# Slot 1 of the routed feed-forward filled from the first three pairs of batches

## The chip, the core and the metric

The kernel runs on one core of a Trainium2 chip. Five engines work on it at once, each through its own list of instructions in order: PE (TensorE, matrix products; its weight loads are shown apart as PEld), DVE (VectorE), ACT (ScalarE), POOL (GpSimd) and SP (SyncE, which issues most of the DMAs). An instruction starts when the one before it on its engine allows it and when the semaphores that it waits for have come. The metric is the device time of one execution in microseconds (us); lower is better. PE's clock has two levels, 2.4 and 1.2 GHz; the profile writes the granted one as a share of the full clock, 1.00 or 0.50, and a mean over a stretch in between.

## What is computed

Attention with two softmaxes, a routed feed-forward with one of 8 experts for each token, and a gated feed-forward over all tokens:

```python
q_s = softmax(q, axis=-1)                    # q, k, v: 8 batches x 8 heads x 576 x 64
k_s = softmax(k, axis=2)                     # over the sequence
kv  = einsum('bhsd,bhse->bhde', k_s, v)
x   = einsum('bhsd,bhde->bhse', q_s, kv)     # -> 4608 tokens x 512
logits = x @ w_gate + modality_bias[modality_id]
e_idx, gate_w = argmax(logits), softmax(logits)[e_idx]
for e in range(8):                           # w1: 8 x 512 x 1024, w2: 8 x 1024 x 512
    out[e_idx == e] = gate_w * (relu(x[e_idx == e] @ w1[e]) @ w2[e])
y = ((out @ w_a) * (out @ w_b)) @ w_out      # w_a, w_b: 512 x 1536, w_out: 1536 x 512
```

## The kernel before

**Stages.** First the attention, in 16 units (`u`: a batch and one half of its heads), software-pipelined by the list `STEP`: in each turn every step runs for another unit. After every second batch (a *pair*: 1152 tokens, 9 columns of 128) the pair is routed. The routing is a generator that `more` advances a few operations at a time among the attention's steps: logits, the one-hot choice `oh`, the rank of each token within its expert (running counts are in `carry`), and for each column two matrices `la` and `lb` that carry the token numbers. When a pair is done, `("route", n)` is set and a hook `then[n]` is called, if there is one.

**Slots.** The routed feed-forward runs in slots of 256 tokens, all of one expert. Each slot gathers its tokens (two indirect DMAs on POOL's queue, `gather`, 128 rows each, from `xd`, the attention's output in DRAM), scales them by row (`xscale` on DVE, four small operations for each half: `xm`, `xp`, `xr`, `fc`; `xmul` on ACT), transposes them on PE (`xtrans`), splits them into a high and a low part of 16 bits (`xsplit`: high on ACT, low on DVE, into `xhl`), multiplies by w1 (`ph`, 96 products; in slot 0 `pt`), makes `hh` (ACT) and `hl` (DVE) of that for each of 8 blocks, multiplies by w2 (`py`; in slot 0 `po`), and scales the sum on ACT (`ysb`) for the store to `yd`. 19 slots run. The *leader* is the expert that has most tokens after the first pair (`plan_first`, `c.first`). Slot 0 takes the first 256 of the leader's tokens and is worked beside the attention's last units, slot 1 the next 256.

**Which tokens are slot 0's and slot 1's.** `Plan.first` decides that. `rank`, called after the second pair, lifts the leader's running count to at least 256 (`max(256, carry)`), so that no later token gets a rank that slot 0 has; how far it was lifted is `phi`. `mark(n, s)` makes a one-hot table `eq` (in the tile `tables`) over the first `n` columns: which leader's tokens have the ranks of slot `s`. `products(n)` multiplies it by `la` and `lb` of each column, 2 `n` small products on PE into `pid`, and `index(s)` turns that into the row numbers `gidx` that the gather reads. For slot 0 `n` is 18 (two pairs); for slot 1 it is 36, all columns, so the chain waits for the last pair's routing. `Plan.tokens` does the same for all other slots, as four times 18 products (`pid<-eqs`).

**What sets the order.** The slot-0 and slot-1 work is cut into chains of small steps; a step is put into the program at a `tick` of the attention once its conditions are in `gone` and the count of ticks has reached its number in the table `AT` (third row: slot 1's chain, whose 15 steps are `mark`, products, `index`, the gather, scaling, transposes and splits). From slot 2 on the class `Work` puts the conversions of weights and the steps of `Plan.tables` (it writes the table of slots, with each slot's base from `phi` and the counts) one by one into the engines' lists, by their costs and due times; another step in its list moves what is behind it.

**After the slots** comes the gated feed-forward (`Gated`), 9 blocks of 512 tokens, which is over half of the time and keeps PE busy.

Some names: `kvb` is the small matrix of a unit that its output products (`po<-kvb,qt`) use, `psg` the sum it comes from; `w_91` and `w_92` are the expert's w1 and w2 in 16 bits, of which DVE makes the low part and POOL, ACT and DVE the high one; `hot` is the one-hot table from which ACT makes `la` and `lb`; `x` and `xs` are the attention's output tiles.

Of the kernel before, what the change touches and what calls it, by code (L numbers as in the profile page):

```python
# [13 lines left out]
ALU = mybir.AluOpType  # L14
AX = mybir.AxisListType
# [4 lines left out]
B, H, S, D = 8, 8, 576, 64  # L20
NTOK = B * S
# [15 lines left out]
class Attention:  # L37
# [368 lines left out]
    def more(self, n):  # L406

        while n > 0 and self.todo is not None:
# [16 lines left out]


# [162 lines left out]
class Plan:  # L589
# [18 lines left out]
    def first(self, at):  # L608

        nc, c, v = self.nc, self.c, self.nc.vector  # L610
        t8, self.phi = self.tile(2, NE), self.tile(1)
        hs, hi = self.tile(NT, NE), self.tile(NT)
        self.hs = hs.rearrange("p n e -> p (n e)")
        eq = self.tile(NT).bitcast(F16).rearrange("p (n two) -> p n two", two=2)

        def rank():
            v.scalar_tensor_tensor(t8[:, 0], c.first, float(SLOT), c.carry, ALU.mult, ALU.max)
            v.tensor_tensor(t8[:, 1], t8[:, 0], c.carry, ALU.subtract)
            v.tensor_copy(c.carry, t8[:, 0])
            v.tensor_reduce(self.phi, t8[:, 1], AX.X, ALU.add)  # L620
            mark(18, 0)

        def mark(n, s):
            v.tensor_tensor(hs[:, 0:n], c.oh[:, 0:n], c.first[:, None, :].to_broadcast([P, n, NE]), ALU.mult)
            v.tensor_reduce(hi[:, 0:n], hs[:, 0:n], AX.X, ALU.add)
            v.scalar_tensor_tensor(hi[:, 0:n], hi[:, 0:n], -1000.0, c.hir[:, 0:n], ALU.mult, ALU.add)
            v.tensor_tensor(eq[:, 0:n], hi[:, 0:n, None].to_broadcast([P, n, 2]),
                            c.is1000[:, None, 2 * s:2 * s + 2].to_broadcast([P, n, 2]), ALU.is_equal)

        def products(n):  # L630
            self.ps = at.ps_t.tile([P, 2], F32, tag="pt", name="pid0")
            for j in range(n):
                nc.tensor.matmul(self.ps, c.la[:, j], eq[:, j], start=j == 0, stop=False)
                nc.tensor.matmul(self.ps, c.lb[:, j], eq[:, j], start=False, stop=j == n - 1)

        def index(s):
            v.tensor_scalar(c.gidx[:, 2 * s:2 * s + 2], self.ps, -65.0, 0.0, ALU.add, ALU.max)

        return (rank, [([("route", 1), ("kmax_t", 13)], lambda: products(18)), ((), lambda: index(0)), ((), lambda: at.gone.add("0"))],
                [([("route", NT // 9 - 1), "0"], lambda: mark(NT, 1)), ((), lambda: products(NT)), ((), lambda: index(1))])  # L640

    def tokens(self, at):

# [45 lines left out]
    def tables(self, done):  # L689
# [48 lines left out]
        v.tensor_reduce(bs, g, AX.X, ALU.add)  # L738
        yield one
        v.scalar_tensor_tensor(bs, c.iota50[:, 0:MAXSLOT], float(SLOT), bs, ALU.mult, ALU.add)  # L740
        yield one
        v.tensor_scalar(c.plan[:, BASE:BASE + MAXSLOT], bs, self.phi, float(NTOK), ALU.subtract, ALU.min)
        yield one
# [111 lines left out]
class Experts:  # L855
# [165 lines left out]
    def gather(self, s, j):  # L1021
        nc, c = self.nc, self.c
        nc.gpsimd.indirect_dma_start(  # L1023
            out=self.x[:, j], out_offset=None, in_=self.xd[0:4 * S if s == 0 else NTOK, :],
            in_offset=bass.IndirectOffsetOnAxis(ap=c.gidx[:, 2 * s + j:2 * s + j + 1], axis=0))

    def xscale(self, h):
# [926 lines left out]
def moe_kernel(ctx: ExitStack, tc: tile.TileContext, q, k, v, mid, wg, mb, w1, w2, wa, wb, wo, out, dbg=None):  # L1954
# [8 lines left out]
    with ExitStack() as ectx:  # L1963
        ex = Experts(tc, ectx, c, xd, yd, wd, w1, w2)
        plan = Plan(tc, ectx, c)
        with ExitStack() as rctx:
            load_modality, token_bias = setup_tokens(tc, rctx, c, mid, wg, mb)
            with ExitStack() as actx:
                at = Attention(tc, actx, c, q, k, v, xd, ex)
                rank, *tokens = plan.first(at)  # L1970
                early = [*ex.early(at, *tokens), plan.tokens(at)]
                at.run({0: [load_modality], 3: [token_bias]}, {0: lambda: plan_first(tc, c, at.one), 1: rank}, early)
        if dbg is not None and dbg.get("stop") == "T":
            return
        gctx = ectx.enter_context(ExitStack())
        with ExitStack() as sctx:
            gt = Gated(tc, gctx, sctx, c, dr, ex, plan, wa, wb, wo, out)
            ex.open(sctx)
            if dbg is not None and dbg.get("stop") == "L":
                return  # L1980

            def planned():
                ex.planned = True

            ex.work.add(plan.tables(planned))
            ex.run(gt)
        if dbg is not None:
            nc.sync.dma_start(out=dbg["x"], in_=xd)
            nc.sync.dma_start(out=dbg["plan"], in_=c.plan)
            nc.sync.dma_start(out=dbg["gidx"], in_=c.gidx)  # L1990
            nc.sync.dma_start(out=dbg["y"], in_=yd[0:NTOK, :])
            if dbg.get("stop") == "B":
                return
        gt.open(gctx)
        gt.run()
# [31 lines left out]
```

## Time and profile before

| | us |
|---|---|
| median of 3 runs | 1415.15 |
| lowest, highest | 1412.2, 1416.22 |
| the profiled execution | 1412.71 |
| its span in the trace | 1410.7 |
| PE busy in the span | 1343.4 (95%) |
| DVE busy | 1051.7 (75%) |
| ACT busy | 676.4 |
| POOL busy | 561.1 |

The span is the trace's own time; 2.0 us of the execution lie around it. A line of the timeline has the start, the duration, the engine, the line of the program, the operation, what it writes and reads, shapes and the count; in brackets the idle time of its engine just before it and what ended that. Products overlap in PE's pipeline, so that the next may start before the end shown.

### The profile page before, as it was taken

Reading aid. Unit: us, or ns where it says so; the run is one execution under the profiler, and the core shown is the slowest. Engines: PE = TensorE matmul, PEld = TensorE weight load, DVE = VectorE, ACT = ScalarE, POOL = GpSimd, SP = SyncE. Lnnn points to the kernel's source line nnn. Section 1 sums busy time; section 2 is a strip of 40 time slices with the busy share of each in tenths; the row PEclk is TensorE's granted clock in tenths of the full one; section 3 lists DMA queues with packets and bytes.
Section 4 is the critical chain, followed back from the end, with each engine's and each line's share of the span. In section 5 each row is a group of like instructions: output and inputs, shape, how many; then the busy total and the mean of one; then the engine's idle time right before and its main releaser. Section 6 shows DMA issues by size and latency. Waiting matters only on the chain.

```text
span 1410.7 us, 29129 instructions
## 1 busy us (share of the span) xinstructions
PE 1343.4 (95%) x11068; PEld 1106.5 (78%) x11068; DVE 1051.7 (75%) x2342; ACT 676.4 (48%) x1625; POOL 561.1 (40%) x696
## 2 busy tenths in 40 slices
PE   6887899999999999999999999999999999999996
PEld 4776776666676776768888888888888888888885
DVE  6889876776787777426777878788787877878755
ACT  4566563764455554323545354454443545454433
POOL 6655431524443354103334343433434334343433
PEclk9988799999999999999999999999999999999999
DMA  9987234789654345117001010100101001010000
GB/s 245 269 261 218 85 129 146 268 310 310 225 199 155 108 135 165 61 47 292 1 18 45 1 61 2 61 1 1 61 1 61 1 17 46 1 61 1 32 1 31
DMA packets 87911, 145.79 MB, mean 103 GB/s; under 512 B 19792, under 2 KB 60752, under 8 KB 85584
## 3 DMA queue, kind: packets, MB, share of 16 engines
q1 hardware_dynamic: 81136, 123.85, 27.2%
q0 software_dynamic: 6080, 19.95, 4.3%
q8 instruction: 90, 1.47, 0.4%
q14 instruction: 61, 0.50, 0.1%
q10 hardware_dynamic: 544, 0.02, 0.0%
HBM read 149.78 MB, written 46.44 MB: 139 GB/s over the span
## 4 chain that ended last, share of the span: by engine, by line
PE 52%; issue 1%; DVE 1%; POOL 1%; ACT 0%; POOLq 0%; DVEq 0%
PE ab L1654 34%; PE mp L1674 17%; PE ab L1338 1%; POOL out_dram L1748 0%; ACT y L1333 0%; POOLq L2022 0%; DVE g L1903 0%; DVE y L1348 0%; POOL raw L1693 0%; DVE w L1903 0%; DVE w L1358 0%; DVE g L1906 0%; DVE gr L1902 0%; POOL gs L1780 0%; POOL w L1693 0%
## 5 line engine op out<-in xcount | busy, mean ns | idle before, releaser
L1654 PEld LDWEIGHTS <-gw 128*128 128x128 f16 x3780 | 369.5, 98 | 53.2 <-issue 8.9
L1654 PE MATMUL ab<-raw,gw 128*128 128x256 f16 x2100 | 280.4, 272 | 3.7 <-DVE w L1906 1.1
L1654 PE MATMUL ab<-w,gw 128*128 128x256 f16 x1680 | 225.2, 273 | 0.2
L1674 PEld LDWEIGHTS <-gp 128*128 128x128 f16 x1944 | 190.0, 98 | 22.6 <-DVE gp L1701 0.8
L1061 PEld LDWEIGHTS <-w 128*128 128x128 f16 x1824 | 179.4, 99 | 31.6 <-issue 6.5
L1061 PE MATMUL ph<-xhl,w 128*128 128x256 f16 x1728 | 195.7, 274 | 4.7 <-DVE hl L1069 2.4
L1078 PE MATMUL py<-w,hh 128*128 128x512 f16 x576 | 171.3, 379 | 0.1
L1674 PE MATMUL mp<-wo,gp 128*128 128x256 f16 x756 | 141.8, 273 | 0.0
L1701 DVE SCALAR_TENSOR_TENSOR gp<-gp,gs 128x256 f16<-128x256 f16 x162 | 88.9, 553 | 36.8 <-ACT gp L1696 36.5
L1069 DVE SCALAR_TENSOR_TENSOR hl<-ph,hh 128x256 f16<-128x256 f32 x144 | 59.1, 420 | 72.7 <-ACT hh L1068 69.5
L1078 PE MATMUL py<-w,hl 128*128 128x512 f16 x288 | 109.1, 379 | 0.0
L1078 PEld LDWEIGHTS <-hh 128*128 128x128 f16 x608 | 59.5, 99 | 61.6 <-issue 0.3
L1470 POOL TENSOR_TENSOR gf<-gf 128x256 f32<-128x256 f32 x72 | 64.1, 910 | 94.7 <-ACT gf L1513 86.2
L1696 ACT ACTIVATE gp<-g 128x256 f16<-128x256 f32 x108 | 45.0, 418 | 98.8 <-DVE g L1906 97.9
L1732 POOL TENSOR_TENSOR gs<-w 128x256 f32<-128x256 f32 x54 | 39.6, 734 | 125.8 <-DVE w L1906 125.8
L1674 PE MATMUL mp<-w,gp 128*128 128x256 f16 x324 | 88.3, 273 | 0.0
L1674 PE MATMUL mp<-raw,gp 128*128 128x256 f16 x324 | 88.3, 273 | 0.0
L1068 ACT ACTIVATE hh<-ph 128x256 f16<-128x256 f32 x144 | 54.3, 379 | 68.3 <-PE ph L1061 67.8
L1701 DVE SCALAR_TENSOR_TENSOR gp<-gp,g 128x256 f16<-128x256 f16 x108 | 74.2, 688 | 15.8 <-ACT gp L1696 15.7
L1023 POOL DMA_INDIRECT xg<-xd,gidx x40 | 44.4, 1111 | 98.6 <-ACT xhl L1052 51.6
L1654 PEld LDWEIGHTS <-w 128*128 128x128 f16 x756 | 73.9, 98 | 10.1 <-issue 0.7
L1893 ACT COPY gr<-ab 128x256 f32<-128x256 f32 x108 | 40.3, 373 | 86.5 <-PE ab L1654 86.0
(358 smaller groups left out, 2740.0 us busy)
## 6 DMA issues: line engine op xcount, KB each, us to landing
w<-wd SPq DMA_DIRECT2D x58, 1024.0 KB
raw<-in_moe_w_dram SPq DMA_DIRECT2D x24, 512.0 KB
yd<-ysb SPq DMA_DIRECT2D x19, 513.0 KB
xd<-x SPq DMA_DIRECT2D x8, 1026.0 KB
y<-yd SPq DMA_DIRECT2D x8, 1026.0 KB
w<-in_k_dram SPq DMA_DIRECT2D x16, 512.0 KB
wd<-wst SPq DMA_DIRECT2D x16, 512.0 KB
g<-in_moe_w_a_dram SPq DMA_DIRECT2D x12, 512.0 KB
```

The lines of the kernel that those rows point to most:

```text
L1023: nc.gpsimd.indirect_dma_start(out=self.x[:, j], out_offset=None, in_=self.xd[0:4 * S if s == 0 else NTOK, :], in_offset=bass.IndirectOffs ...
L1061: nc.tensor.matmul(ph, self.w1[:, w, k, o], x[:, k], start=i == 0, stop=i == 11)
L1068: nc.scalar.activation(self.hh[:, f], ph, AF.Relu)
L1069: nc.vector.scalar_tensor_tensor(self.hl[:, f], ph, 0.0, self.hh[:, f], ALU.max, ALU.subtract)
L1078: nc.tensor.matmul(self.py[j], h[:, f, o], self.w2[:, w, f], start=f == 0 and i == 0, stop=f == 7 and i == 2)
L1470: self.nc.gpsimd.tensor_tensor(s[:, dst], s[:, x], s[:, y], ALU.subtract)
L1654: self.nc.tensor.matmul(ps, self.w[f][:, b, o:o + P], self.y[n].op[:, a, yl, 256 * k:256 * k + 256], start=i == 0 and fresh, stop=i == 5, ...
L1674: self.nc.tensor.matmul(onto[:, t], x, y, start=start and j == 0, stop=i == last and t == 1 and j == 2, skip_group_check=nm == "p3" and al ...
L1696: self.nc.scalar.activation(self.part(i, a)[:, 0], x, AF.Copy, scale=2.0 ** -11)
L1701: eng.scalar_tensor_tensor(p[:, 1], p[:, 0], -2048.0, x, ALU.mult, ALU.add)
L1732: pool.tensor_tensor(x, a11, a21, ALU.subtract)
L1893: nc.scalar.copy(r, x)
```

## The change

The running count of the leader is shifted a second time, after the third pair: `later` lifts it to at least 512, by the same four operations as `rank` (`shift(s)`), and adds the two lifts (`gap`) up to `phi`. With that, slot 1's ranks lie within the first three pairs. `mark` and `products` of slot 1 run over 27 columns, not 36, and wait for the third pair's routing, not the last one's; its gather reads rows of the first 6 batches only. The third row of `AT` has earlier numbers, and `Plan.tables` adds slot 1's own lift to its base, which is one more step in `Work`'s list.

With this input the leader has 595 tokens after the first pair and 1146 after the third: both lifts are zero, and slot 1 gets the same tokens as before.

```diff
--- before.py
+++ after.py
@@ -420,7 +420,7 @@
           (505, 509, 509, 509, 509, 552, 557, 565, 574, 574, 587, 596, 619, 623, 643, 648, 649, 650, 650, 653,
            654, 660, 667, 667, 668, 668, 668, 668, 670, 670, 670, 676, 676, 676, 679, 679, 679, 679,
            679, 696, 738, 765),
-          (643, 643, 648, 653, 691, 694, 696, 702, 702, 711, 711, 711, 715, 715, 740),
+          (618, 622, 628, 648, 650, 660, 665, 668, 671, 677, 677, 678, 680, 681, 683),
           (637, 659, 662, 704, 708, 714, 714, 714, 714, 718, 724))
 
 
@@ -608,17 +608,24 @@
     def first(self, at):
 
         nc, c, v = self.nc, self.c, self.nc.vector
-        t8, self.phi = self.tile(2, NE), self.tile(1)
+        t8, self.phi, self.gap = self.tile(2, NE), self.tile(1), self.tile(2)
         hs, hi = self.tile(NT, NE), self.tile(NT)
         self.hs = hs.rearrange("p n e -> p (n e)")
         eq = self.tile(NT).bitcast(F16).rearrange("p (n two) -> p n two", two=2)
 
-        def rank():
-            v.scalar_tensor_tensor(t8[:, 0], c.first, float(SLOT), c.carry, ALU.mult, ALU.max)
+        def shift(s):
+            v.scalar_tensor_tensor(t8[:, 0], c.first, float(SLOT * (s + 1)), c.carry, ALU.mult, ALU.max)
             v.tensor_tensor(t8[:, 1], t8[:, 0], c.carry, ALU.subtract)
             v.tensor_copy(c.carry, t8[:, 0])
-            v.tensor_reduce(self.phi, t8[:, 1], AX.X, ALU.add)
+            v.tensor_reduce(self.gap[:, s:s + 1], t8[:, 1], AX.X, ALU.add)
+
+        def rank():
+            shift(0)
             mark(18, 0)
+
+        def later():
+            shift(1)
+            v.tensor_reduce(self.phi, self.gap, AX.X, ALU.add)
 
         def mark(n, s):
             v.tensor_tensor(hs[:, 0:n], c.oh[:, 0:n], c.first[:, None, :].to_broadcast([P, n, NE]), ALU.mult)
@@ -636,8 +643,8 @@
         def index(s):
             v.tensor_scalar(c.gidx[:, 2 * s:2 * s + 2], self.ps, -65.0, 0.0, ALU.add, ALU.max)
 
-        return (rank, [([("route", 1), ("kmax_t", 13)], lambda: products(18)), ((), lambda: index(0)), ((), lambda: at.gone.add("0"))],
-                [([("route", NT // 9 - 1), "0"], lambda: mark(NT, 1)), ((), lambda: products(NT)), ((), lambda: index(1))])
+        return (rank, later, [([("route", 1), ("kmax_t", 13)], lambda: products(18)), ((), lambda: index(0)), ((), lambda: at.gone.add("0"))],
+                [([("route", 2), "0"], lambda: mark(27, 1)), ((), lambda: products(27)), ((), lambda: index(1))])
 
     def tokens(self, at):
 
@@ -738,6 +745,8 @@
         v.tensor_reduce(bs, g, AX.X, ALU.add)
         yield one
         v.scalar_tensor_tensor(bs, c.iota50[:, 0:MAXSLOT], float(SLOT), bs, ALU.mult, ALU.add)
+        yield one
+        v.tensor_tensor(bs[:, 1:2], bs[:, 1:2], self.gap[:, 1:2], ALU.add)
         yield one
         v.tensor_scalar(c.plan[:, BASE:BASE + MAXSLOT], bs, self.phi, float(NTOK), ALU.subtract, ALU.min)
         yield one
@@ -1021,7 +1030,7 @@
     def gather(self, s, j):
         nc, c = self.nc, self.c
         nc.gpsimd.indirect_dma_start(
-            out=self.x[:, j], out_offset=None, in_=self.xd[0:4 * S if s == 0 else NTOK, :],
+            out=self.x[:, j], out_offset=None, in_=self.xd[0:(4 + 2 * s) * S if s < 2 else NTOK, :],
             in_offset=bass.IndirectOffsetOnAxis(ap=c.gidx[:, 2 * s + j:2 * s + j + 1], axis=0))
 
     def xscale(self, h):
@@ -1967,9 +1976,9 @@
             load_modality, token_bias = setup_tokens(tc, rctx, c, mid, wg, mb)
             with ExitStack() as actx:
                 at = Attention(tc, actx, c, q, k, v, xd, ex)
-                rank, *tokens = plan.first(at)
+                rank, later, *tokens = plan.first(at)
                 early = [*ex.early(at, *tokens), plan.tokens(at)]
-                at.run({0: [load_modality], 3: [token_bias]}, {0: lambda: plan_first(tc, c, at.one), 1: rank}, early)
+                at.run({0: [load_modality], 3: [token_bias]}, {0: lambda: plan_first(tc, c, at.one), 1: rank, 2: later}, early)
         if dbg is not None and dbg.get("stop") == "T":
             return
         gctx = ectx.enter_context(ExitStack())
```

Where the instructions stand. PE at the attention's last unit (`kvb_189` is that unit's, `kvb_185` the one's before it), before:

```order
L306 MATMUL po<-kvb_185,qt 128x146 x4
L100 MATMUL pt<-ident,kvb_189 128x128 x2
L246 MATMUL psg<-wgbd,kt 128x16 x2
L306 MATMUL po<-kvb_189,qt 128x146 x8
L1061 LDWEIGHTS w_91
L1061 MATMUL pt<-xhl,w_91 128x256
```

and now:

```order
L306 MATMUL po<-kvb_185,qt 128x146 x4
L100 MATMUL pt<-ident,kvb_189 128x128 x2
L246 MATMUL psg<-wgbd,kt 128x16 x2
L640 LDWEIGHTS la
L640 MATMUL pid_2137<-tables,la 128x2
L641 LDWEIGHTS lb
L641 MATMUL pid_2137<-tables,lb 128x2
...
L641 MATMUL pid_2137<-tables,lb 128x2
L306 MATMUL po<-kvb_189,qt 128x146 x8
L1070 LDWEIGHTS w_91
L1070 MATMUL pt<-xhl,w_91 128x256
```

The 54 products of slot 1's table stand between the sum for `kvb_189` and the attention's last products but those of `shared` (`L640` is line 633 of before).

DVE at the same place, before:

```order
L225 TENSOR_SCALAR rd<-pk 128x2
L226 RECIPROCAL rd<-rd 128x2
L230 TENSOR_TENSOR kvb_189<-pk,rd 64x2x64 x2
L284 TENSOR_SCALAR rc<-po 128x2x4
L285 RECIPROCAL rc<-rc 128x2x4
L286 TENSOR_TENSOR x_2073<-po,rc 128x2x256
L1050 TENSOR_TENSOR xhl<-po,xhl 128x512
L841 SCALAR_TENSOR_TENSOR w_92<-raw_90,est_114,w_92 128x1024
```

and now:

```order
L225 TENSOR_SCALAR rd<-pk 128x2
L226 RECIPROCAL rd<-rd 128x2
L230 TENSOR_TENSOR kvb_189<-pk,rd 64x2x64 x2
L284 TENSOR_SCALAR rc<-po 128x2x4
L285 RECIPROCAL rc<-rc 128x2x4
L286 TENSOR_TENSOR x_2073<-po,rc 128x2x256
L631 TENSOR_TENSOR tables<-oh,first 128x216
L632 TENSOR_REDUCE tables<-tables 128x27
L633 SCALAR_TENSOR_TENSOR tables<-tables,hir 128x27
L634 TENSOR_TENSOR tables<-tables,is_81 128x54
L1059 TENSOR_TENSOR xhl<-po,xhl 128x512
L644 TENSOR_SCALAR gidx<-pid_2137 128x2
L850 SCALAR_TENSOR_TENSOR w_92<-raw_90,est_114,w_92 128x1024
```

The four operations of `mark` stand ahead of the second low part of slot 0's tokens, and `index` right behind that part. The five operations of the second shift stand some rows earlier, ahead of the unit before's evacuation.

DVE in the last pair's routing, beside slot 0's first layer, before:

```order
L376 TENSOR_REDUCE rk<-eq 128x9
L1069 SCALAR_TENSOR_TENSOR hl<-pt,hh 128x256
L378 TENSOR_REDUCE g<-ex 128x9
L380 TENSOR_SCALAR hir<-rk 128x9
L381 TENSOR_SCALAR g<-g 128x9
L382 TENSOR_SCALAR hir<-hir 128x9
L383 RECIPROCAL g<-g 128x9
L385 SCALAR_TENSOR_TENSOR rf<-hir,rk 128x9
L841 SCALAR_TENSOR_TENSOR w_92<-raw_90,est_114,w_92 128x1024
L397 TENSOR_TENSOR hot<-iota_127,rf 128x1152
L1069 SCALAR_TENSOR_TENSOR hl<-pt,hh 128x256 x3
L841 SCALAR_TENSOR_TENSOR w_92<-raw_90,est_114,w_92 128x1024
```

and now:

```order
L376 TENSOR_REDUCE rk<-eq 128x9
L1078 SCALAR_TENSOR_TENSOR hl<-pt,hh 128x256
L855 TENSOR_REDUCE xm_99<-xg 128x1
L860 TENSOR_SCALAR xp_107<-xm_99 128x1
L850 SCALAR_TENSOR_TENSOR w_92<-raw_90,est_114,w_92 128x1024
L397 TENSOR_TENSOR hot<-iota_127,rf 128x1152
L1078 SCALAR_TENSOR_TENSOR hl<-pt,hh 128x256 x3
L855 TENSOR_REDUCE xm_99<-xg 128x1
L860 TENSOR_SCALAR xp_107<-xm_99 128x1
L861 RECIPROCAL xr_101<-xp_107 128x1
L1042 TENSOR_TENSOR fc_103<-xp_107,xg 128x1
L850 SCALAR_TENSOR_TENSOR w_92<-raw_90,est_114,w_92 128x1024
L1078 SCALAR_TENSOR_TENSOR hl<-pt,hh 128x256
```

The two halves' scaling of slot 1's tokens, which stood behind the tables of the other slots, stands once ahead of the routing's `g` and once behind three of slot 0's `hl`. POOL at the same place, before:

```order
L292 TENSOR_TENSOR lraw<-lraw,rc 128x256
L292 TENSOR_TENSOR lraw<-lraw,rc 128x64
L837 TENSOR_SCALAR w_92<-raw_90,est_114 128x1024
L389 COPY x_1844<-g 128x4
L389 COPY x_2073<-g 128x4
L392 COPY xs_2164<-g 128x1
L1023 DMA xg<-xd,gidx 128x513 x2
L1091 COPY ysb<-gidx 128x2
```

and now:

```order
L292 TENSOR_TENSOR lraw<-lraw,rc 128x256
L292 TENSOR_TENSOR lraw<-lraw,rc 128x64
L1032 DMA xg<-xd,gidx 128x513 x2
L846 TENSOR_SCALAR w_92<-raw_90,est_114 128x1024
L389 COPY x_1844<-g 128x4
L389 COPY x_2073<-g 128x4
L392 COPY xs_2229<-g 128x1
L1100 COPY ysb<-gidx 128x2
```

Slot 1's two gathers stand ahead of the last conversion of `w_92` and of the last pair's copies, not behind them.

On PE slot 1's eight transposes stand behind six of the eight groups of the first half of slot 0's w2 products, where before they stood among the `pid<-eqs` products behind the second half; the 72 products of its table are gone from behind six groups of that first half. In slot 1 SP's loads of `w_b` and `w_out` stand ahead of those of the slot table, where before they stood behind them, and the conversions of weights in slots 2 and 3 stand elsewhere by a few rows.

## Rows read from the trace of the kernel before

**Rows 1.** Timeline of PE at the end of slot 0 and the start of slot 1, and of slot 6.

```profile
219.21 0.38 PE L1078 MATMUL po<-w,hl 128*128 128x512 f16 x1
...
221.11 0.66 PE L1044 MATMUL po<-ident,xg 128*128 128x128 f32 x4 [1.06 <-ACT xg L1036]
...
226.42 12.53 PE L1061 MATMUL ph<-xhl,w 128*128 128x256 f16 x96 [1.13 <-ACT ysb L1093]
...
343.33 10.64 PE L1061 MATMUL ph<-xhl,w 128*128 128x256 f16 x96
```

**Rows 2.** Timeline of Pool and DVE between slots 0 and 1.

```profile
215.59 1.05 POOL L1023 DMA_INDIRECT xg<-xd,gidx  x1 [9.85 <-DVE plsm L669]
...
219.18 0.69 DVE L846 TENSOR_REDUCE xm<-xg 128x1 f32<-128x512 f32 x1 [2.85 <-DMA xg<-xd,gidx]
...
220.17 0.14 DVE L1033 TENSOR_TENSOR fc<-xp,xg 128x1 f32<-128x1 f32 x1
```

**Rows 3.** Busy time by stretch; the third number from the right is the granted clock.

```profile
219.00:222.00 3.00, 1.71 (x25) 1.13 (x23) 2.54 (x10) 0.98 (x2) 0.00 (x0) 1.00 0.18 70
...
228.00:230.00 2.00, 2.00 (x12) 1.39 (x10) 0.67 (x4) 0.38 (x1) 0.74 (x1) 0.50 0.98 192
```

**Rows 4.** Timeline of PE, DVE and Pool around the attention's last units.

```profile
190.34 0.62 PE L246 MATMUL psg<-wgbd,kt 128*128 128x16 f32 x4 [0.46 <-ACT kt L240]
...
191.24 2.26 PE L306 MATMUL po<-kvb,qt 128*128 128x146 f32 x16 [0.28 <-ACT kvb L249]
...
186.98 0.17 DVE L284 TENSOR_SCALAR rc<-po 128x8 f32<-128x8 f32 x1 [1.55 <-ACT lraw L276]
...
190.92 0.68 DVE L1050 TENSOR_TENSOR xhl<-po,xhl 128x512 f16<-128x512 f32 x1
...
194.37 0.63 POOL L292 TENSOR_TENSOR lraw<-lraw,rc 128x256 f32<-128x256 f32 x1 [9.47 <-DVE rc L285]
```

**Rows 5.** Timeline of DVE and PE: slot 1's one-hot table and its products.

```profile
208.80 0.45 DVE L624 TENSOR_TENSOR tables<-oh,first 128x288 f32<-128x288 f16 x1
...
210.00 0.23 DVE L627 TENSOR_TENSOR tables<-tables,is 128x72 f16<-128x72 f32 x1
...
211.15 0.17 PE L633 MATMUL pid<-tables,la 128*128 128x2 f16 x1
...
212.93 0.16 PE L634 MATMUL pid<-tables,lb 128*128 128x2 f16 x1
```

**Rows 6.** Timeline of DVE and PE in slot 0's first layer.

```profile
205.49 0.42 DVE L1069 SCALAR_TENSOR_TENSOR hl<-pt,hh 128x256 f16<-128x256 f32 x1
...
205.96 1.47 PE L1061 MATMUL pt<-xhl,w 128*128 128x256 f16 x12 [0.62 <-DVE hl L1069]
```

**Rows 7.** Landing of slot 0's gathers, of all gathers, and the stores of finished slots.

```profile
DMA to landing us min/median/max: 4.6/4.6/4.6
...
DMA to landing us min/median/max: 3.6/5.7/8.4
...
L1097 SPq DMA_DIRECT2D yd<-ysb x19: 373/399/922, 226.4 to 631.0; - x19
```

**Rows 8.** Timeline of DVE and Pool where the first shift runs.

```profile
134.66 2.69 DVE L619 COPY carry<-tables 128x8 f32<-128x8 f32 x1
...
135.25 2.07 POOL L200 TENSOR_TENSOR qr<-q,mq 128x512 f32<-128x512 f32 x2
```

**Rows 9.** Busy time by stretch where the clock fell or held.

```profile
130.00:136.00 6.00, 4.83 (x25) 4.38 (x24) 5.93 (x6) 6.00 (x20) 3.90 (x4) 0.72 1.07 199
...
160.00:162.00 2.00, 1.20 (x10) 1.21 (x11) 1.78 (x3) 1.80 (x7) 1.39 (x3) 1.00 0.80 195
...
168.00:170.00 2.00, 0.57 (x3) 0.60 (x4) 1.82 (x8) 0.00 (x0) 0.00 (x0) 0.72 0.02 4
...
168.00:176.00 8.00, 6.17 (x29) 5.72 (x29) 5.99 (x19) 5.09 (x11) 1.51 (x2) 0.57 0.00 1
```

**Rows 10.** Busy time by stretch in slots 2 and 3.

```profile
260.00:282.00 22.00, 18.68 (x121) 11.70 (x120) 21.59 (x37) 12.86 (x24) 16.51 (x14) 1.00 0.63 216
```

## The prediction

> **What bounds the kernel now.** I read the page first, then busy time by stretch, then the timelines of PE, DVE and POOL from the attention's last units into slot 1. PE is busy for 1343.4 of 1410.7 us, so the end moves only by what PE is made to wait, to do, or to do at its lower clock. [rows 1] show one place where it does both. Slot 0's last product issues at 219.21; slot 1's transposes wait 1.06 us for ACT's scaling, and slot 1's first products wait another 1.13 us at 226.42. The scaling is late because its tokens are [rows 2]: POOL issues the gather only at 215.59, and DVE waits 2.85 us for it to land, until 219.18. In that gap the clock falls: PE is busy 1.71 of 3 us in 219 to 222, and in 228 to 230 the granted clock is 0.50, the 1.2 GHz level [rows 3]. The 96 products that begin slot 1 take 12.53 us where those of slot 6, without a fall, take 10.64 [rows 1]. So 1.06 + 1.13 us of waits and 12.53 − 10.64 = 1.89 us of low clock are at stake here, and nothing else that the change aims at: from slot 2 on, tokens come by another chain.
>
> Nothing here is hidden behind a DMA: the store of finished slots has 19 rows [rows 7], one for each slot that runs, and both lifts of the counts are zero with this input, so slot 1 has the same tokens and there is no slot more or less.
>
> **The change part by part.** The times are those of the profiled execution, 1412.71 us, which is 2.4 under the median of the three runs; I carry a difference over to both.
>
> (a) *Slot 1's table and products beside the attention's last unit.* On DVE `mark` with 36 columns runs from 208.80 to 210.00 + 0.23 = 210.23, 1.43 us [rows 5]. With 27 columns the two large operations are three quarters as long, and I take 1.25. It stands where the second low part began, at 190.92 [rows 4], so the table is ready at about 192.2. PE stands behind it: the sum for the last unit starts at 190.34 for 0.62 us [rows 4], then 54 products wait. At a pitch of (212.93 − 211.15) / 71 = 25 ns [rows 5] they take 1.35 us, and the attention's last output products, which started at 191.24, start at 193.6: **2.4 us later** than before. Behind them queue all of slot 0's products and, through the evacuations, the last pair's routing. DVE's chain from there is back to back, and shifts by the same 2.4. Bounds: zero, if the table came in DVE's gaps, and 2.6, with the full 1.43.
>
> The second shift is five operations on 8 columns, about 0.85 us if each takes 0.17 like `rc` [rows 4], and DVE waits 1.55 us ahead of 186.98 for ACT [rows 4], where they stand. I cost it at nothing. If that cover is gone, its bound is the first shift: one copy of it took 2.69 us at 134.66, while POOL had an operation from 135.25 [rows 8]; with the other four some 4.5.
>
> (b) *Slot 1's scaling in the routing.* One half is 219.18 to 220.17 + 0.14, 1.13 us [rows 2]. The first half stands ahead of `g`, `hot` and the `hl` of block 4. That `hl`, at 205.49 before, comes 2.4 + 1.13 = 3.5 us later, and the products of slot 0's block 7, which waited 0.62 us for it at 205.96 [rows 6], now wait about 1.75. So slot 0's w2 products start 3.5 later. The second half stands ahead of the last `hl`, which the w2 products need only some 4 us after their start; it has that room and costs nothing. If it hadn't, it would be 1.13.
>
> (c) *The end of slot 0.* Its last product ended at 219.21 + 0.38 = 219.6. Later by 3.5, less the 72 products that go (72 x 25 ns = 1.8), plus the eight transposes that now stand inside (four took 0.66 [rows 1]; eight about 1.0): 222.3. The transposes stand behind the same six groups of products as the 72 did, so they are due at 211.15 + 3.5 = 214.7 [rows 5]; DVE's second half of the scaling follows three `hl` that stand 3.5 later than at 205.49 to 207.3, so that ends about 212, and ACT adds one operation. They don't wait.
>
> (d) *The junction.* The 72 products for the other slots' tokens are left, all in one go, at the same pitch about 1.8 us; the splits of slot 1's transposes run meanwhile. Slot 1's first product starts at about 224.1, not 226.42: **−2.3 us**. The waits of 1.06 and 1.13 are gone from here; what they were is partly paid in (a) and (b).
>
> (e) *The clock in slot 1.* PE now has no gap from block 7 on, so slot 1 should run at the full level: **−1.9 us** [rows 1]. Bounds 0 and −1.9.
>
> (f) *The clock earlier.* There are two new waits, 1.3 us ahead of the 54 products (after 0.46 that was there) and 1.75 at block 7. What a gap of that size does, the rows tell only by neighbours. In 160 to 162 PE was busy 1.20 of 2 and the clock held at 1.00; in 168 to 170 it was busy 0.57 of 2 and the clock fell, and it is 0.57 as a mean of 168 to 176, which is (1 − 0.57) x 8 / 0.5 = 6.9 us at the low level; in 130 to 136 it is 0.72, 3.4 us at the low level [rows 9]. The new waits leave PE busier than in 168 to 170 and are nearest to the row that held, but there are two, and beside each PE has shorter gaps. I take one fall of 3.4 us, with half of that lost: **+1.7**. Bounds 0 and 6.9 (both fall for 6.9 us, half lost).
>
> (g) *The gather.* On POOL it now follows the operations that ended at about 197.6 (the first of them stands at 194.37 [rows 4]) and issues about 200. Slot 0's took 4.6 us from issue to landing [rows 7], so it lands at 204.6, when DVE comes to it: `hl` at 205.49 [rows 6] has two long and six short routing operations ahead of it, some 3.1 us, so the scaling stands at 202.4, plus 2.4. No wait. All gathers took 3.6 to 8.4 [rows 7]; at the long end DVE waits 3.6 more, and all behind it does. On POOL the last conversion of `w_92` and the copies of the last pair stand behind the two issues, some 2.3 us; what DVE needs of them comes later still.
>
> (h) *The plan.* One small operation more, and conversions in slots 2 and 3 in other places. In 260 to 282 PE is busy 18.68 of 22 us and DVE 21.59 [rows 10]: DVE is the bound there, and another order can give or take a wait. No row tells which; I take 0, with −2 and +2 as bounds, which is more than half of PE's 3.3 idle us there.
>
> Sum: −2.3 − 1.9 + 1.7 = **−2.5 us**: 1410.2 in the profiled execution's terms, 1412.6 against the median.
>
> A rule of the Trainium skill speaks against where the shift and `mark` stand. What the trace shows is [rows 8]: a copy of 8 columns took 2.69 us while POOL worked. The skill's page "SBUF — State Buffer", section "SBUF: two separate sides", says that DVE and GpSimd share one port pair as an exclusive lock, held for a whole instruction, so that the loser is blocked; the row agrees. By that rule the change is dear if POOL works at 184 to 192 and free if not. POOL is idle there, 9.47 us up to 194.37 [rows 4], so by row and rule the sum stays as it is; the case in which POOL works there all the same is rival D.
>
> **The rivals.**
>
> *B, the clock holds in both new waits.* For it: the row 160 to 162, at 1.20 busy of 2, held. Against: two waits, the longer with little work of long products around it. The sum is without (f): −4.2, and with some relief in slots 2 and 3 up to −6: 1410.9, down to 1409.
>
> *C, the clock falls in both and stays low as in 168 to 176.* One mechanism: the waits that the change puts ahead of the 54 products and of block 7 cost the clock that it wins in slot 1. Price 2 x 6.9 / 2 = 6.9: −4.2 + 6.9 = +2.7, 1417.9, slower than before. It decides from the point where both stretches show 0.50 for over 4.2 us each. For it: [rows 3], where 1.29 us of idle in 3 lost the clock. Against: the row that held.
>
> *D, DVE is blocked.* POOL, pushed by other arrivals, works while the shift or `mark` runs, and these take as long as the first shift: the shift 4.5 − 0.85 − its cover of 0.7 = 3 more, `mark` 2.4 more, for which all of PE waits. −2.5 + 5.4 = +2.9: 1418. Against: POOL's 9.47 idle us, which end on DVE's own work.
>
> *E, it doesn't do what it says:* the gather isn't earlier, or there is a slot more (some 21 us). The counts and the conditions exclude both, except that the gather's landing may stretch, (g).
>
> **How the numbers follow.** A 0.43, B 0.34, C 0.16, D with a late gather 0.07. The predicted time is A's, 1412.6. The range runs from 1409.0, B with its relief, to 1417.2, which takes in the better half of C and A with (h) at its bad end; about 2 in 10 lie outside. A measurement of this kernel can tell about 0.3% (4.2 us) from no change. B's centre lies on that bound, and with slot 2 and 3's relief and its share of A's spread I give faster 0.29; slower by that much needs C or D and a loss in (h) on top: 0.11; the rest, 0.60, is within.
>
> **What the profile of the changed kernel would show.** (a): 54 products at about 192.3 with an idle of 1.3 us ahead, released by DVE's table. (b): 1.75 us idle ahead of block 7, released by `hl`. (d): slot 1's first `ph` at about 224.1, no wait for `xg` or `ysb`. (e): granted clock 1.00 in slot 1, and 96 products in 10.6 us. (f): the granted clock in the 8 us after each of the two waits; 1.00 in both is B, 0.50 for long in both is C. (g): POOL's gather at about 200. (h): PE's waits in 260 to 282. Wrong would be any of: operations of the shift or `mark` of over 1 us, DVE waiting for the gather in the routing, or more than 19 stores.

## The result and the profile after

| | before | changed |
|---|---|---|
| median of the 7 runs of each beside one another (us) | 1415.15 | 1422.2 |
| lowest, highest | 1412.2, 1416.54 | 1418.35, 1425.86 |
| span of the profiled execution | 1410.7 | 1420.4 |

The changed kernel is slower: ratio 1.006, interval 1.0048 to 1.0072. The forecast was 1412.6 with a range up to 1417.2.

Where the time goes is seen first from SP's stores of finished slots, the 3rd to 6th after slot 0's (slots 3 to 6), in the timeline of the kernel before and then of the changed one. Columns: start, duration, engine, line, what is written and read.

```profile
300.53 0.51 SPq L1097 DMA_DIRECT2D yd<-ysb  x1
...
325.75 0.37 SPq L1097 DMA_DIRECT2D yd<-ysb  x1
...
345.05 0.92 SPq L1097 DMA_DIRECT2D yd<-ysb  x1
...
366.46 0.39 SPq L1097 DMA_DIRECT2D yd<-ysb  x1
```

```profile
301.25 0.41 SPq L1106 DMA_DIRECT2D yd<-ysb  x1
...
330.69 0.37 SPq L1106 DMA_DIRECT2D yd<-ysb  x1
...
349.41 0.39 SPq L1106 DMA_DIRECT2D yd<-ysb  x1
...
376.33 0.39 SPq L1106 DMA_DIRECT2D yd<-ysb  x1
```

From slot 3's store to slot 4's it is 29.4 us where it was 25.2, and from slot 5's to slot 6's 26.9 where it was 21.4: 4.2 and 5.5 us more. Slot 1's store had been 0.4 earlier than before and slot 3's 0.7 later, and from slot 6's, 9.9 later, on nothing is added but 0.2. So the part of the program that the change is about ends slightly ahead, and most of the loss lies in two slots behind it.

**The part up to slot 1**, in the timeline of PE of the changed kernel, with the rows that answer to [rows 1, 4, 6]:

```profile
191.24 0.62 PE L246 MATMUL psg<-wgbd,kt 128*128 128x16 f32 x4 [0.46 <-ACT kt L240]
...
193.12 0.16 PE L640 MATMUL pid<-tables,la 128*128 128x2 f16 x1 [1.27 <-DVE tables L634]
...
194.49 3.83 PE L306 MATMUL po<-kvb,qt 128*128 128x146 f32 x16
...
207.06 0.19 PE L364 MATMUL psr<-oh,tri 128*128 128x72 f16 x1 [1.32 <-DVE oh L358]
...
213.15 1.47 PE L1070 MATMUL pt<-xhl,w 128*128 128x256 f16 x12 [1.66 <-DVE hl L1078]
...
228.04 10.65 PE L1070 MATMUL ph<-xhl,w 128*128 128x256 f16 x96 [0.31 <-DVE gidx L689]
```

The last unit's sum starts 0.9 us later than before. Of that difference 0.8 is there already at 100 us of the span, ahead of everything that the change touches, and in other executions the sum starts up to 4 us later (below), so all stretches here are counted from this sum on. The 54 products wait 1.27 us for their table; the attention's last products come 2.35 us later than before relative to the sum, and they take 3.83 us instead of 2.26. Then PE waits 1.32 us for DVE's one-hot choice `oh`, which it did not do before, and 1.66 at block 7. Slot 1's 96 products take 10.65 us, as in slot 6 before. Counted from the sum to slot 1's store it is 250.78 − 191.24 = 59.5 us, before 251.20 − 190.34 = 60.9.

The clock shows why the last products took longer; busy time by stretch of the changed kernel (third number from the right):

```profile
194.00:196.00 2.00, 2.00 (x31) 2.00 (x28) 1.34 (x2) 0.00 (x0) 0.00 (x0) 0.58 0.04 8
...
196.00:198.00 2.00, 2.00 (x11) 2.00 (x10) 0.88 (x4) 0.21 (x1) 0.00 (x0) 0.56 0.00 0
...
198.00:200.00 2.00, 2.00 (x23) 1.64 (x22) 1.53 (x5) 0.21 (x1) 0.63 (x1) 1.00 0.00 0
...
212.00:214.00 2.00, 0.85 (x8) 0.77 (x8) 1.31 (x3) 1.21 (x5) 1.05 (x3) 1.00 0.85 353
```

After the first new wait the clock is low for (0.42 + 0.44) x 2 / 0.5 = 3.4 us. After the two later ones, for `oh` and at block 7, it held at 1.00.

**DVE's one-hot choice** was late because one comparison took 1.60 us. Timelines of DVE and POOL, first of the kernel before and then of the changed one:

```profile
200.10 0.22 DVE L354 SCALAR_TENSOR_TENSOR eq<-L,w 128x72 f32<-128x72 f32 x1
...
197.58 1.12 POOL L837 TENSOR_SCALAR w<-raw,est 128x1024 f16<-128x1024 f32 x1
```

```profile
204.38 0.23 DVE L352 TENSOR_TENSOR L<-L,mxl 128x72 f32<-128x72 f32 x1
...
204.87 1.60 DVE L354 SCALAR_TENSOR_TENSOR eq<-L,w 128x72 f32<-128x72 f32 x1
...
204.27 0.95 POOL L1032 DMA_INDIRECT xg<-xd,gidx  x1 [0.30 <-issue]
...
205.25 1.13 POOL L846 TENSOR_SCALAR w<-raw,est 128x1024 f16<-128x1024 f32 x1
```

Before, POOL's conversion of `w` ended 1.4 us ahead of the comparison. Now it follows the gathers, starts during the comparison and ends at 206.38, and the comparison, which reads two operands from SBUF, ends 0.1 us after it. By these records the comparison began 0.38 us ahead of the conversion, more than the 0.22 us that it needs, while POOL still issued the second gather. What held it so long is not shown. The operation ahead of it, `L<-L,mxl`, which also reads two operands, began and ended beside the same gather and took 0.23 us.

**Slot 4.** PE's transposes for the next slot wait twice, and the clock falls behind them. Timelines of PE, DVE and ACT and busy time by stretch of the changed kernel:

```profile
315.31 0.33 PE L1053 MATMUL pxt<-ident,xg 128*128 128x128 f32 x1 [1.63 <-ACT xg L1045]
...
317.23 1.75 PE L1053 MATMUL pxt<-ident,xg 128*128 128x128 f32 x7 [1.59 <-ACT xg L1045]
...
310.76 1.22 DVE L855 TENSOR_REDUCE xm<-xg 128x2 f32<-128x1024 f32 x1 [4.16 <-DMA xg<-xd,gidx]
...
312.70 0.15 DVE L958 TENSOR_REDUCE est<-st 128x2 f32<-128x8 f32 x1
...
313.50 1.15 ACT L844 ACTIVATE wst<-raw,est 128x1024 f16<-128x1024 f32 x1 [4.59 <-DVE est L962]
...
314.55 0.70 ACT L1045 ACTIVATE xg<-xg,xr 128x512 f32<-128x512 f32 x1
...
318.00:320.00 2.00, 2.00 (x8) 1.16 (x7) 2.00 (x3) 1.14 (x4) 0.00 (x0) 0.50 0.18 68
```

DVE waits 4.16 us for the gathered tokens, and the scale `est` of the next expert's weights is queued behind that. ACT has a conversion with that scale ahead of its scaling of the tokens (`xg`), waits for it until 313.50, and PE waits for ACT. In the kernel before DVE has the same two in the other order:

```profile
305.74 0.15 DVE L949 TENSOR_REDUCE est<-st 128x2 f32<-128x8 f32 x1
...
308.96 1.22 DVE L846 TENSOR_REDUCE xm<-xg 128x2 f32<-128x1024 f32 x1 [2.40 <-DMA xg<-xd,gidx]
```

**Slot 6.** PE stops behind the 23rd of the 96 products, and from 352 to 354 no engine works. Timeline of PE and busy time by stretch of the changed kernel:

```profile
348.77 2.68 PE L1070 MATMUL ph<-xhl,w 128*128 128x256 f16 x23 [0.28 <-ACT ysb L1102]
...
354.31 9.80 PE L1070 MATMUL ph<-xhl,w 128*128 128x256 f16 x73 [2.86 <-issue]
...
352.00:354.00 2.00, 0.00 (x0) 0.00 (x0) 0.00 (x0) 0.00 (x0) 0.00 (x0) 1.00 1.03 410
...
354.00:356.00 2.00, 1.69 (x11) 1.27 (x11) 0.42 (x1) 0.38 (x1) 0.00 (x0) 0.69 1.02 404
...
356.00:358.00 2.00, 2.00 (x11) 1.45 (x10) 0.42 (x1) 0.38 (x1) 0.00 (x0) 0.50 1.04 315
```

"issue" means that the profile shows nothing that PE waited for. The DMA engines are full (1.03). When PE goes on, the clock is low for about 3.4 us.

### The profile page after: what moved, and what is told of

Same layout as the page of the kernel before. It is cut to its first block, busy times and chain, and to the rows that moved or that the text cites. A ratio compares the mean times of both kernels' runs of the same rounds, so it can differ in the third digit from the quotient of the medians.

```text
span 1420.4 us, 29100 instructions
## 1 busy us (share of the span) xinstructions
PE 1346.9 (95%) x11050; PEld 1108.2 (78%) x11050; DVE 1056.3 (74%) x2348; ACT 676.1 (48%) x1625; POOL 561.3 (40%) x696
## 4 chain that ended last, share of the span: by engine, by line
PE 51%; issue 1%; DVE 1%; POOL 1%; ACT 0%; POOLq 0%; DVEq 0%; ACTq 0%
PE ab L1663 34%; PE mp L1683 16%; PE ab L1347 1%; POOL out_dram L1757 0%; DVE gp L1710 0%; ACT y L1342 0%; POOL raw L1702 0%; POOL gs L1741 0%; POOLq L2031 0%; DVE y L1357 0%; DVE w L1912 0%; DVE w L1367 0%; POOL gs L1789 0%; DVE gu L1908 0%; POOL w L1702 0%
## 5 line engine op out<-in xcount | busy, mean ns | idle before, releaser
L1683 PEld LDWEIGHTS <-gp 128*128 128x128 f16 x1944 | 190.0, 98 | 22.7 <-DVE gp L1710 0.8
```

Source lines behind the costliest of these rows:

```text
L1683: self.nc.tensor.matmul(onto[:, t], x, y, start=start and j == 0, stop=i == last and t == 1 and j == 2, skip_group_check=nm == "p3" and al ...
```

## The experiments

Theory P puts the losses behind slot 1 down to the one more step in the planner's list, Q to the arrivals that the early products shift. The first two kernels do the halves of the change alone. Where a stretch is given, "sum to slot 1" runs from the attention's last sum to slot 1's store (before: 60.9 us), "slot 4" from slot 3's store to slot 4's (25.2), "slot 6" from slot 5's to slot 6's (21.4), each from one profiled execution.

**e1, the early part alone.** The step is folded into the one ahead of it:

```diff
         v.scalar_tensor_tensor(bs, c.iota50[:, 0:MAXSLOT], float(SLOT), bs, ALU.mult, ALU.add)
-        yield one
         v.tensor_tensor(bs[:, 1:2], bs[:, 1:2], self.gap[:, 1:2], ALU.add)
```

> The changed kernel, but the slot table's new small operation stands in the step before it, so that the later order of conversions and loads is that of before; the early products, the second shift and the early gather stay. Theory P (the one step more in the planner's list costs the time: the losses of 4.2 us in slot 4 and 5.5 us at slot 6 follow from its order): both losses go, slot 1's store stays at -0.4 against before, and the span is about 1410.7, ratio to before 1.000. Theory Q (the early products shift the slots in time, and that makes gathers and weights late): both losses stay, span about 1420, ratio 1.006.

Measured: ratio 1.0012 (1.0001 to 1.0023), span 1414.1. Sum to slot 1 59.9, slot 4 25.7: that loss is gone. Slot 6 22.7: the stop is still there, 1.66 us.

**e2, the step alone.**

```diff
         v.scalar_tensor_tensor(bs, c.iota50[:, 0:MAXSLOT], float(SLOT), bs, ALU.mult, ALU.add)
         yield one
+        v.tensor_scalar(bs[:, 1:2], bs[:, 1:2], 0.0, None, ALU.add)
+        yield one
```

> The kernel before, with one small operation (adding zero to slot 1's base) as a step of its own in the planner's list, and nothing else of the change. Theory P: the losses in slots 4 and 6 come, span about 1420, ratio 1.007. Theory Q: nothing changes, ratio 1.000.

Measured: ratio 1.0025 (1.0012 to 1.0037), span 1417.7. Slot 4 28.6: the loss is there, with 3.4 us of waits of the transposes for `xg`. Slot 6 21.8, no stop. So neither theory holds for both losses: slot 4's belongs to the step, slot 6's stop to the early part, with which alone it costs 1.3 of the 5.5 us.

**e3 and e4, two places in the early part.** In the row of `AT`, mark, products and index of slot 1 (e3), and its two gathers (e4), both from e1:

```diff
-          (618, 622, 628, 648, 650, 660, 665, 668, 671, 677, 677, 678, 680, 681, 683),
+          (628, 636, 637, 648, 650, 660, 665, 668, 671, 677, 677, 678, 680, 681, 683),
```

```diff
-          (618, 622, 628, 648, 650, 660, 665, 668, 671, 677, 677, 678, 680, 681, 683),
+          (618, 622, 628, 660, 660, 660, 665, 668, 671, 677, 677, 678, 680, 681, 683),
```

> e1 with slot 1's table one DVE operation later and its 54 products behind the attention's last output products. If the wait of 1.5 us ahead of the products and the fall of the clock behind it (1.6 us) are what the early place costs: no such wait, no fall, slot 1's first product some 3 to 4 us earlier than in e1 (about 224), ratio to before 0.997. Rival: DVE's four table operations are the cost wherever they stand, and the later gather makes DVE wait in the routing: under 1 us earlier than e1.

Measured: ratio 0.9992 (0.9979 to 1.0005). The wait ahead of the products is gone and the clock is 1.00 from 190 to 202; sum to slot 1 58.1, 1.8 us less than e1, half of what was expected. `mark`'s four operations (0.19 to 0.38 us each) still stand in DVE's chain ahead of the last evacuations; that they are the other half is not shown, since no kernel here has them elsewhere. The stop in slot 6 is there, 1.75 us, and slot 4 takes 26.8 (in e4 26.5), 0.8 to 1.1 more than in e1, which no run explains.

> e1 with slot 1's two gathers behind POOL's last conversion of w2, as before. Theory L (DVE's comparison in the routing took 1.60 us, not 0.23, since POOL converted beside it): it takes 0.23 again, and PE's wait of 1.3 us for the one-hot choice goes; the gather issues 1.1 us later, so DVE may wait up to 1.1 us for it ahead of the scaling: together 0.3 to 1.4 us less than e1. Rival: the comparison is slow for another reason: still 1.6 us, and e4 is equal to e1 or up to 1.1 us slower.

Measured: ratio 1.0002 (0.9992 to 1.0012). Timelines of DVE and POOL of e4:

```profile
208.00 0.22 DVE L354 SCALAR_TENSOR_TENSOR eq<-L,w 128x72 f32<-128x72 f32 x1
...
205.47 1.12 POOL L845 TENSOR_SCALAR w<-raw,est 128x1024 f16<-128x1024 f32 x1
...
206.75 1.05 POOL L1031 DMA_INDIRECT xg<-xd,gidx  x1 [0.15 <-PE pt L1069]
...
208.10 0.95 POOL L1031 DMA_INDIRECT xg<-xd,gidx  x1 [0.30 <-issue]
```

With the conversion out of its way the comparison takes 0.22 us, and PE doesn't wait for `oh`. DVE doesn't wait for the tokens either. Sum to slot 1 58.3, 1.6 less than e1. So DVE's operation is held until POOL's conversion ends. That the issue of a gather doesn't hold it is not shown by this row, since the comparison starts between the two issues; `L<-L,mxl` above, of the same size, was not held by one. By the Trainium skill's page "SBUF — State Buffer", section "SBUF: two separate sides", a DVE operation with two SBUF inputs and a GpSimd operation that reads SBUF exclude each other for a whole instruction, the first to start going first. The end of the comparison, 0.1 us after the conversion's, agrees with that; its recorded start, ahead of the conversion's, does not.

**e5, e6: is the stop a matter of PE's own list?** In e1, e3, e4 and the changed kernel it stands behind the same 23rd product (the expectations call it the 24th; in the changed kernel 24 weight loads stand ahead of the stop), PE goes on at 347.6 to 354.3 us of the span, and in before and e2 there is no stop. Common to the four is that PE's list has 36 rows less (54 products with their loads, not 72). The instructions themselves come over the DMA engines too (rows "instruction" of the queues). So 18 products are added whose sum is thrown away:

```diff
+            for j in range(9 if n == 27 else 0):
+                nc.tensor.matmul(self.ps, c.la[:, j], eq[:, j], start=j == 0, stop=False)
+                nc.tensor.matmul(self.ps, c.lb[:, j], eq[:, j], start=False, stop=j == 8)
             for j in range(n):
```

> e1 with 18 products more (9 columns once ahead of slot 1's products, their sum is thrown away), so that every later instruction stands at the same place of PE's list as in the kernel before. Theory C (PE's stop without a releaser in slot 6, always behind the same 24th product, is the arrival of PE's own instructions over full DMA engines; with 36 rows less the border falls elsewhere): no stop there; slot 5's store to slot 6's takes 21.4 us as before, not 22.7; ratio to before about 1.000. Rival: the stop is a late load of slot 6's weights, which the earlier slots cause: it stays at 1.4 to 1.7 us.

Measured: no stop, slot 6 21.0, slot 4 25.3; ratio 1.0006 (0.9994 to 1.0017). This is the early part without either of the two losses, but for 0.5 us of added products, and it is not faster than the kernel before: sum to slot 1 60.9, as there, with the clock low for 6.8 us behind the first new wait.

> The changed kernel with the same 18 products more. Theory C: the stop of 2.86 us in slot 6 and the fall of the clock behind it go, 5.5 us less between the stores of slots 5 and 6 (21.4, not 26.9); slot 4's loss of 4.2 us, which comes from the planner's order, stays: ratio to before 1.003. Rival (late weights, since slot 4's loss delays their stores): the stop stays, ratio 1.006.

Measured: no stop, slot 6 21.8; slot 4 28.9; ratio 1.004 (1.0027 to 1.0053).

**e10, the stop alone.** The kernel before with slot 1's products over 27 columns:

```diff
-        [([("route", NT // 9 - 1), "0"], lambda: mark(NT, 1)), ((), lambda: products(NT)), ((), lambda: index(1))])
+        [([("route", NT // 9 - 1), "0"], lambda: mark(NT, 1)), ((), lambda: products(27)), ((), lambda: index(1))])
```

> The kernel before, with slot 1's products over 27 columns instead of 36 (its tokens lie in the first three pairs with this input): 36 rows of PE's list less, and nothing else of the change. Theory C (PE's instructions arrive late at a fixed place of its list): a stop of 1.4 to 2.9 us without a releaser behind the 24th product of slot 6, so 1 to 5 us between the stores of slots 5 and 6 more than before's 21.4, against 0.45 us won by the products: ratio 1.001 to 1.003. Rival: the stop belongs to the early products' arrivals: no stop, ratio 1.000.

Measured: ratio 1.0014 (0.9999 to 1.003), slot 6 22.5. Timeline of PE of e10, of e5, and the row of the DMA queue that carries instructions in the half microsecond from 343.0 of e10 and from 352.0 of the changed kernel (packets, MB, share of the engines):

```profile
341.85 2.57 PE L1061 MATMUL ph<-xhl,w 128*128 128x256 f16 x22
...
345.78 8.24 PE L1061 MATMUL ph<-xhl,w 128*128 128x256 f16 x74 [1.36 <-issue]
...
344.20 10.64 PE L1072 MATMUL ph<-xhl,w 128*128 128x256 f16 x96
```

```profile
q8 instruction: 1, 0.02, 11.8%
```

```profile
q8 instruction: 1, 0.02, 11.8%
```

The stop, here one product earlier, comes with nothing of the change but the shorter list. In the changed kernel, e1, e3, e4 and e10 PE goes on 2.3 to 2.9 us after the start of the half microsecond in which that queue moved its packet (347.0 and 349.46 in e1, 352.0 and 354.31 in the changed kernel). In e7 below, whose stop is the shortest, it is 3.5 us (344.5 and 348.05), so the distance is not fixed. Such a packet also comes without a stop, at 344.0 in before and at 345.0 in e5, so that the coincidence says little by itself. What is shown is that the stop hangs on the length of PE's list; that PE waited for its instructions is read from that and from the place, and the trace has no row that says so.

**e7, slot 4.** The changed kernel, with the next slot's scaling one step later in slot 4:

```diff
-                if t == 6:
+                if t == (7 if s == 4 else 6):
                     do("dve", 1.5, self.xscale, None)
```

> The changed kernel with one edit: in slot 4 the scaling of the next slot's tokens on DVE stands one step later, so that the weights' scales stand ahead of it, as in the kernel before. Theory S (in slot 4 DVE waits 4.2 us for the gather with the scales queued behind it, so ACT's conversions and behind them its scaling of the tokens come late, and PE's transposes wait twice for 1.6 us): the waits of the transposes go to under 1 us, and slot 3's to slot 4's store takes about 25.5 us, not 29.4; slot 6's stop stays: ratio to before 1.003. Rival: the gather's landing alone is late: the waits stay within 1 us of what they were.

Measured: the transposes wait 0.7 us at most and slot 4 takes 26.3, 3.1 less. But slot 5 takes 22.2 (18.7 in the changed kernel), 2.0 of it a wait of the second layer for its weights, and slot 6 stops for 0.51 only. Ratio 1.0025 (1.0014 to 1.0036). The order of `est` and the scaling was the cause in slot 4. What it gave there was paid again in slot 5; what e7 wins over the changed kernel is the shorter stop, slot 6 in 21.0.

**e8, all four mended**: e1, e3's and e4's numbers in `AT`, and e5's products.

> The change with four edits: the new step folded into its neighbour (e1), the products behind the attention's last output products (e3), the gathers behind POOL's conversion (e4), and 18 products for PE's place (e5). If the four costs are apart from each other: from the attention's last unit to slot 1's store 60.9 - 2.8 - 1.3 = 56.8 us, no stop in slot 6, slot 4 within 1.5 us of before: 2.5 to 4 us less than before, ratio 0.997 to 0.998. Rival: what is won ahead of slot 2 is lost again in slots 4 to 6, where DMA and DVE are full: ratio 1.000.

Measured: ratio 0.9982 (0.997 to 0.9994), sum to slot 1 56.9, slot 4 25.7, slot 6 21.4, no stop. Up to slot 1 the costs add up as expected (56.8).

**e9, the scaling.** e8 with the first half of slot 1's scaling behind three `hl`, the second behind the last.

```diff
-          (628, 636, 637, 660, 660, 660, 665, 668, 671, 677, 677, 678, 680, 681, 683),
+          (628, 636, 637, 660, 660, 668, 671, 671, 671, 677, 677, 678, 680, 681, 683),
```

> e8 with the first half of slot 1's scaling moved from ahead of the routing's last part to behind three of slot 0's hl, the second half behind the last hl. The prediction's term (b): the scaling ahead of block 4's hl costs PE 1.13 us at block 7. If so, that wait falls from 1.7 to about 0.6 us and the stretch from the attention's last unit to slot 1's store is 1.1 us shorter than in e8; ratio to before about 0.9975. Rival: the tokens are scaled too late for the transposes, which then wait as long: equal to e8.

Measured: the wait at block 7 is 0.62, not 1.66; sum to slot 1 56.1; ratio 0.9983 (0.9973 to 0.9992). In the profiled executions it is 0.8 shorter than e8 in this stretch; as a whole the two can't be told apart.

## Where the prediction was right and where it was wrong

**(a), (f), first wait.** Right: 54 products with 1.27 us ahead of them (1.3), the last products 2.35 later (2.4), one fall of the clock of 3.4 us (3.4) that cost 3.83 − 2.26 = 1.6 us (1.7), and no second fall at block 7. e3 shows that place and fall go together. The size was in part luck: in e5, with the same wait, the clock was low for 6.8 us, and in e10 PE was busy for only 0.46 of 2 us (220 to 222), less than in the row of [rows 9] that fell, and it held.

**(b), (c).** Right: 1.66 at block 7 (1.75), and e9 gives 1.04 of it back (1.13). The transposes didn't wait.

**(e)** came as forecast, slot 1 at the full clock (10.65), but the 1.9 us were no fixed price of the order before. e2 has the same order as before up to there and e10 only 18 small products less. Their waits ahead of slot 1 are longer than before's, and yet their 96 products take 10.64. Timelines of PE and busy time by stretch, first of e2, then of e10:

```profile
229.59 10.64 PE L1063 MATMUL ph<-xhl,w 128*128 128x256 f16 x96 [0.99 <-DVE xhl L1052]
...
226.00:228.00 2.00, 2.00 (x46) 2.00 (x45) 0.73 (x2) 0.99 (x2) 0.00 (x0) 0.50 0.04 8
```

```profile
227.22 10.64 PE L1061 MATMUL ph<-xhl,w 128*128 128x256 f16 x96 [1.83 <-ACT ysb L1093]
...
220.00:222.00 2.00, 0.46 (x12) 0.35 (x9) 1.66 (x6) 0.72 (x1) 0.00 (x0) 1.00 0.24 94
...
224.00:226.00 2.00, 1.40 (x54) 1.28 (x49) 1.15 (x3) 1.17 (x3) 0.00 (x0) 1.00 0.00 0
```

In e2 the clock fell earlier, under the small products, and in e10 not at all. So the sum to slot 1 is 60.9, 60.1 and 59.0 with before's order, and 59.5, 59.9, 59.6, 60.9 and 59.9 in the changed kernel, e1, e7, e5 and e6: that the early part as the change has it wins anything is not shown. The bound of 0 that (e) names would have been as good a term.

**(d).** Slot 1's first product came at 228.04, less the 0.9 that is older than the change 227.1, not 224.1. Of the 3.0, 1.6 is the fall of the clock, which the sum has in (f). The rest is about the comparison's 1.60 us for 0.22; smaller differences cancel.

**The missed step there is (g)**: it moved the gathers past POOL's conversion and asked only what of the conversion's result is needed when. It did not ask what the conversion runs beside. That was rival D's mechanism, tied to the shift and to `mark`, where POOL was idle as forecast (the five operations of the shift took 0.15 to 0.17 us each). The sum with it is −2.5 + 1.4 = −1.1 up to slot 1; measured 59.5 − 60.9, −1.3, from the sum to slot 1's store, in these two executions.

**(h) was wrong, and decides the case.** One step more in the planner's list was taken at 0 with bounds of 2 us, read from slots 2 and 3 [rows 10]. In these slots it cost 1.1 us (1.3 in e2). In slot 4, where I had not looked, it cost 4.2 (3.4 in e2), with a mechanism that the order shows: DVE's `est` on the other side of an operation that waits for a DMA, and ACT's list in the way of PE's transposes. A bound for a changed order had to be read from every slot in which the order differs, by the waits that stand in its queues.

**What the sum did not have at all** is PE's shorter list, 5.5 us in the changed kernel and 1.1 to 1.4 in e1, e3, e4 and e10. The 72 products that go were booked as 1.8 us won. Why the stop is longer in the changed kernel (2.86, and a fall of the clock behind it) than in e1 (1.66) stays open; both stand under full DMA engines. It is also the larger part of why e1 and e2 together (0.12% and 0.25%) are less than the whole (0.6%): slot 6 loses 1.3 and 0.4 us in them, and 5.5 in the whole.

None of the rivals was the case that came: C's clock fell once, not twice, and D struck elsewhere.

## What to carry to other kernels

When a change moves a DMA or a conversion past another one on POOL, look at what DVE does beside the moved operation, not only at who needs its result. When code sits under a planner that orders by steps and room, one more step is a change to everything behind it: compare the order there and read the bounds from all of it, or fold the step into another. Here the part that was meant ended 1.3 us ahead in one profiled execution, where e10, with all but before's order, ended 1.9 ahead, and the rest lost 10.5; with four small edits the same idea is 0.18% faster than the kernel before (e8, 0.06 to 0.30%). And a loss to a low clock that one execution shows is not yet a price: take it from several.

## What the runs showed of the hardware that I had not expected

Taking 36 rows out of PE's list made PE stop for 0.5 to 2.9 us some 130 to 160 us later, behind the 22nd or 23rd product of slot 6, with the DMA engines at 0.84 to 1.09; putting 36 rows back removed it (e5, e6), and taking them out of the kernel before brought it (e10). And the time at which the attention's last unit is reached differs by 4 us between executions of kernels that are alike up to there but for the five operations of the shift (190.3 to 194.5), which is more than most of the costs that were looked for: they could be read only as stretches within one execution.
